# The query work of a fused attention and relu² kernel planned by session, and the copy of its sums set between two subtractions

## The chip, the cores and the metric

The kernel runs on one core of a Trainium2 chip. The metric is the device time of one execution in microseconds (us). Runs of the kernel before the change took 1959.41 to 1961.84 us. TensorE is called PE in the profile (PEld is its weight load), VectorE is DVE, ScalarE is ACT, GpSimd is POOL, and SyncE, whose queue issues all the DMAs here, is SP.

## The reference, cut to what matters

```python
# q, k, v: 4 x 12480 x 128; agents: 4 x 49 x 128; w_in: 128 x 2048; w_out: 2048 x 128
def sm(a, b):                                   # softmax of scaled scores
    s = scale * (a @ b.transpose(0, 2, 1))
    e = np.exp(s - s.max(-1, keepdims=True))
    return e / (e.sum(-1, keepdims=True) + 1e-9)
agent_v = sm(agents, k) @ v                     # 4 x 49 x 128
x = (sm(q, agents) @ agent_v).reshape(49920, 128)
h = np.maximum(x @ w_in, 0)
return (h * h) @ w_out
```

The work has two parts for each of the four batches. A small table comes from agents, keys, values and `w_in`: the product of `agent_v` with `w_in`, 49 rows of 2048. Then each token needs only its 49 softmax weights times that table, relu, square, and the product with `w_out`.

## The kernel before, in words

The 49920 tokens are 52 blocks of 960 (13 to a batch), and a block is two halves of G = 480 tokens. The 2048 hidden units are 16 chunks of 128, and a slot is two of them for one half, so a half has 8 slots and a block 16. Slots are taken in sessions of 3, 3 and 2 (`SIZES`; the first half of all has four sessions of 2, `EARLY`). In what follows the three sessions of a half are called A, B (three slots each) and C (two slots).

A session `s` does this, in the order of the loop at the end of the kernel. `first` issues the matmuls `h<-w,aw_hi` and `h<-x,aw_ex` of its slots into PSUM and ACT's relu `r<-h` behind them. ACT squares `r` in place (`squares`). `halved` splits the squares of the session before into a rounded part `g_hi` (a cast on DVE) and a rest `g_lo` (a subtraction on DVE). `second` issues, for the session two before (`LAG` = 2), six matmuls a slot into the sum `o`: four with `g_hi` and then, when all of these are out, two with `g_lo`. So PE's order is first(s), second(s-2), first(s+1), second(s-1), and so on: first(A), second(B of the half before), first(B), second(C of the half before), first(C), second(A).

The sum `o` has one PSUM bank. When the second(C) that ends a half is out, `copied_out` copies `o` to `ob` on DVE and sends it to memory; the next half's second(A) may write `o` only when that copy is done. Before the change `copied_out` is called in the session after, so that on DVE the copy stands behind the whole subtraction `g_lo` of session A and ahead of the cast of session B.

Two kinds of work lie beside these sessions. Both are generators, advanced a step at a time: `queries(g)` (the softmax weights of block `g`) and `background(b)` (the table of the next batch from its keys and values; the last batch has none to prepare). Both use one PSUM bank `psa`, one user at a time, and a step of the background that a session takes stands between that session's first and second on PE. The steps of `queries(g)`:

- the load of the block's queries (`qt`);
- the scores `psa<-ag,qt` on PE, with the row maxima `m` and the difference `e` on DVE (L317, L319);
- the exponential on ACT (L323);
- the sums, reciprocal and product on DVE (L326 to L329);
- the cast `pp` on ACT (L227) and its rest on DVE (L229);
- for each half j: four matmuls `psa<-identr,pp`, called transposes below, and the cast `w<-psa` on ACT; in the step after, one DMA `w<-w` (L346) and four DMAs `x<-w` (L348).

Relu, square, the cast `w<-psa`, `g_hi`, `g_lo`, the copy `ob` and all of these matmuls are issued through `queued`, which fixes their order on their engine. The other DVE, ACT and DMA instructions are placed among them by the framework's scheduler.

Before the change `between(k)`, `first` and `due()` decide when the queries advance: the scores of block g+1 in session A of the first half of block g, the steps after it one at each slot, the transposes of j = 0 at the end of A and those of j = 1 at the end of B in the second half of block g. The DMAs follow a slot later.

Of the kernel before, what the change touches and what calls it, by code (L numbers as in the profile page):

```python
# [9 lines left out]
F32 = mybir.dt.float32  # L10
# [13 lines left out]
SIZES = (3, 3, 2)  # L24
EARLY = (2, 2, 2, 2)
WIDEST = max(SIZES)
# [3 lines left out]
LAG = 2  # L30
# [7 lines left out]
BEGIN = 4  # L38
FIRST = 7
# [3 lines left out]
def agent_attention_relu2(ctx: ExitStack, tc: tile.TileContext, qT, kT, v, agT, w_in, w_out, outT):  # L43
# [26 lines left out]
    class Ordered:  # L70
        def __init__(self, eng, always=False):
            self.eng, self.always = eng, always
# [179 lines left out]
    def values(b, i, vt):  # L252
        st = state[b]
        _, rows, nt = blocks[i]
        es = st["mx"][:rows, :nt, :]
        e = small.tile([P, NT, NA], F32, name="d", bufs=2)[:rows, :nt, :] if i else es
        less_maximum(b, i, e, spare())
        yield
        act.activation(e, e, AF.Exp, scale=scale)
        yield 3 if i else FIRST  # L260
        pv = bank()
        for t in range(nt):
            tiled(pv[:C, :NA], vt[:rows, t, :], e[:, t, :], start=(t == 0), stop=(t == nt - 1))
        if i == 0:
            st["av"] = small.tile([C, NA], F32, name="av")
            dve.tensor_copy(st["av"], pv[:C, :NA])
        else:
            dve.tensor_add(st["av"], st["av"], pv[:C, :NA])  # L268
            spare().tensor_add(es, es, e)
# [20 lines left out]
                sync.dma_start(ex[t * 32 : t * 32 + NL, n, :].bitcast(F32), lo[SP:, t * P : (t + 1) * P].bitcast(F32))  # L290


    class Turn:
        def __init__(self, wait):
            self.session = session[0] + wait

    def due():
        at = stands.get("ahead")
        return isinstance(at, Turn) and session[0] >= at.session

    session = [0]
    weights = {}
    slot = [0]

    def queries(g):
        b = g // NB
        qt = qp.tile([C, BLK], F32, name="qt", bufs=1)
        sync.dma_start(qt, qT[:, g * BLK : (g + 1) * BLK])
        yield 3
        ps = ps_a.tile([P, 512], F32, name="psa")  # L310
        sv = ps[:TP, : NT * NA].rearrange("p (t a) -> p t a", a=NA)
        for t in range(NT):
            tiled(sv[:, t, :], qt[:, t * TP : (t + 1) * TP], ag[:, b, :])
        if alone[0]:
            yield
        m = qp.tile([TP, NT, 1], F32, name="m", bufs=1)
        dve.reduce_max(m, sv, axis=AX.X)  # L317
        e = qp.tile([TP, NT, NA], F32, name="e", bufs=1)
        dve.tensor_sub(e, sv, m.broadcast_to([TP, NT, NA]))  # L319
        yield  # L320
        if not alone[0]:
            yield
        act.activation(e, e, AF.Exp, scale=scale)  # L323
        yield
        z = qp.tile([TP, NT, 1], F32, name="z", bufs=1)
        dve.reduce_sum(z, e, axis=AX.X)  # L326
        dve.tensor_scalar_add(z, z, 1e-9)  # L327
        dve.reciprocal(z, z)
        spare().tensor_mul(e, e, z.broadcast_to([TP, NT, NA]))  # L329
        yield  # L330
        pp = qp.tile([TP, NT, K2], F32R, name="pp", bufs=1)
        yield from halves(pp, e, NA, spare())
        weights[g] = []
        for j in range(2):
            yield Turn(0 if j or slot[0] < SLOTS else 2)
            pt = ps_a.tile([P, 512], F32, name="psa")
            for t in range(NT // 2):
                queued(
                    nc.tensor.matmul, nc.tensor, pt[:K2, t * TP : (t + 1) * TP], pp[:, j * (NT // 2) + t, :], identr, start=True, stop=True
                )  # L340
            w = qp.tile([P, G], F32R, name=f"w{j}", bufs=2)
            x = qp.tile([P, G], F32R, name=f"x{j}", bufs=2)
            fixed.copy(w[:K2, :], pt[:K2, :G])
            weights[g].append((w, x))
            yield
            sync.dma_start(w[K2:, :].bitcast(F32), w[:SP, :].bitcast(F32))  # L346
            for t in range(NQ):
                sync.dma_start(x[t * 32 : t * 32 + NL, :].bitcast(F32), w[SP:NA, :].bitcast(F32))  # L348
# [9 lines left out]
    def first(k, m):  # L358

        g, i = divmod(k, SLOTS)  # L360
        j, c = divmod(i, NP)
        b = g // NB
        w, x = weights[g][j]
        hs = [ps_h.tile([P, 2, 512], F32, name="h") for _ in range(m)]
        outs = [(2 * c + n, hs[n // 2][:, n % 2, :G]) for n in range(2 * m)]
        for n, out in outs:
            cs = slice(n * P, (n + 1) * P)
            queued(nc.tensor.matmul, nc.tensor, out, state[b]["hi"][:, cs], w, start=True, stop=False)

        with tc.high_priority():  # L370
            for n, out in outs:
                t = n % NQ
                rows = slice(t * 32, t * 32 + NL)
                queued(nc.tensor.matmul, nc.tensor, out, state[b]["lo"][rows, n // NQ, :], x[rows, :], start=False, stop=True)
        r = ffn.tile([P, WIDEST, 2, G], F32, name="r", bufs=RB)
        for x, h in enumerate(hs):
            queued(nc.scalar.activation, nc.scalar, r[:, x, :, :], h[:, :, :G], AF.Relu)
        for name in ("ahead", "todo"):
            if (m == WIDEST or not due()) and type(stands.get(name)) is int and k >= stands[name] and done[name] < goal[name]:
                move(name, k)  # L380
                break
        return r

    def squares(m, r, apart):
# [6 lines left out]
    def halved(k, m, r, apart):  # L391
        hi = ffn.tile([P, WIDEST, 2, G], F32R, name="g_hi", bufs=HB)
        lo = ffn.tile([P, WIDEST, 2, G], F32R, name="g_lo", bufs=LB)
        for x in pieces(m, apart):
            queued(nc.vector.tensor_copy, nc.vector, hi[:, x, :, :], r[:, x, :, :])
        for x in pieces(m, apart):
            queued(nc.vector.tensor_sub, nc.vector, lo[:, x, :, :], r[:, x, :, :], hi[:, x, :, :].bitcast(F32))
        for x in range(m):
            parts[k + x] = hi[:, x, :, :], lo[:, x, :, :]

    whole_sum = []

# [55 lines left out]
            return next(gen, "end")  # L458

    gens, stands = {}, {}  # L460
    done, goal = {"todo": 0, "ahead": 0}, {"ahead": math.inf}

    def move(name, k):
        done[name] += 1
        said = step(gens[name])
        stands[name] = k + said if type(said) is int else said
# [54 lines left out]
    with tc.tile_pool(name="pre", bufs=PRE) as pre, tc.tile_pool(name="dec", bufs=2) as dec:  # L521
# [48 lines left out]
        asks(2 * FF - WIDE)  # L570
        ahead = queries(1)
        next(ahead)
        gens["todo"], gens["ahead"] = background(1), ahead
        next(gens["todo"])
        stands["todo"], done["todo"], stands["ahead"] = None, 1, BEGIN

        mx = pre.tile([P, 512], F32, name="mx0", bufs=1)
        ss = []
# [121 lines left out]
    def between(k):  # L700
        g, c = divmod(k, SLOTS)
        b, i = divmod(g, NB)
        slot[0] = k
        if b > 0 and i == 0 and c == 0 and b + 1 < B:
            gens["todo"] = background(b + 1)
            stands["todo"], done["todo"] = None, 0
        goal["todo"] = (i * SLOTS + c + 1) * STEPS / (SPREAD * NB * SLOTS) if k >= BEGIN else 0
        while done["todo"] < goal["todo"] and stands["todo"] is None:
            move("todo", k)
        if c == SLOTS // 2 and g < B * NB - 2:  # L710
            following[0] = queries(g + 2)
            step(following[0])
        if c == 0 and 0 < g < B * NB - 1:
            gens["ahead"], stands["ahead"] = following[0], k
        if stands["ahead"] is None and k > 0:
            move("ahead", k)

    following = [None]
    sessions, at = [], 0
    while at < total:  # L720
        for m in SIZES if at else EARLY:
            sessions.append((at, m))
            at += m
    made, split = {}, {}
    for s in range(len(sessions) + LAG):
        k, m = sessions[s] if s < len(sessions) else (total, 0)
        session[0] = s
        if s == LAG:
            behind = [chain[eng] for eng in (nc.tensor, nc.sync, nc.scalar, nc.vector, nc.gpsimd)]
        if m:  # L730
            between(k)
            made[s] = first(k, m)
        copied_out()
        if m:
            squares(m, made[s], s < LAG)
            if s < LAG:
                alone[0] = True
                if s:
                    warm(ps_a, 5)
                table(s + 2)  # L740
                alone[0] = False
        if 1 <= s <= len(sessions):
            halved(*sessions[s - 1], made.pop(s - 1), s <= LAG)
        if s >= LAG:
            second(*sessions[s - LAG])
            if due():
                move("ahead", slot[0])
        for x in range(1, m):
            between(k + x)
    copied_out()  # L750


_NAMES = ["qT", "kT", "v", "agT", "w_in", "w_out"]
# [32 lines left out]
```

## Time and profile before

| what | value |
|---|---|
| median of 3 runs | 1960.92 us |
| profiled execution, its own time | 1959.76 us |
| its span (first to last instruction) | 1957.7 us |
| PE busy | 1902.4 us (97% of the span) |
| PEld busy | 1479.6 us (76%) |
| DVE busy | 1641.2 us (84%) |
| ACT busy | 1628.1 us (83%) |
| mean granted TensorE clock | 0.996 of full speed |

The span is what the trace covers; the profiled execution took 2.1 us more than it. Busy time is the time in which at least one instruction of the engine is running, so 1957.7 less 1902.4 is the time in which PE ran no matmul. Lines of helpers (L64) hold most instructions, so that groups are told apart by their tiles.

### The profile page before, as it was taken

The numbers are of one execution on the slowest core, as the hardware profiler recorded it, in microseconds if no ns is written. First come the engines' busy times: TensorE is split into PE (matmuls) and PEld (weight loads), VectorE is DVE, ScalarE is ACT, GpSimd is POOL, SyncE is SP. The second block draws the span as 40 slices with busy tenths as digits, with TensorE's granted clock in tenths as the row PEclk, the third lists the DMA queues.
The fourth block names the chain that finished last, engine by engine and source line by source line (L and its number), as shares of the span: only waits on it lengthen the run. The fifth ranks groups of instructions, "written<-read, shape, count | busy, mean of one in ns | idle before, by whom it ended". The sixth has DMA issues, their size and how long they took to land.

```text
span 1957.7 us, 39753 instructions
## 1 busy us (share of the span) xinstructions
PE 1902.4 (97%) x17181; PEld 1479.6 (76%) x17181; DVE 1641.2 (84%) x1371; ACT 1628.1 (83%) x1516; POOL 20.7 (1%) x24
## 2 busy tenths in 40 slices
PE   7899999999999999999999999999999999999999
PEld 4677777777777777777777777777777777777777
DVE  7778888888888888888888888888888888888887
ACT  5778788888888888888888888888888888889886
POOL 2100000000000000000000000000000000000000
PEclk9999999999999999999999999999999999999999
DMA  9222122122122222122112221222111111111100
GB/s 373 78 87 90 55 62 78 62 65 68 37 64 91 72 64 73 56 74 67 56 47 74 78 76 41 67 72 75 47 39 51 36 51 34 45 43 40 47 22 27
DMA packets 54819, 131.47 MB, mean 67 GB/s; under 512 B 6508, under 2 KB 34828, under 8 KB 54644
## 3 DMA queue, kind: packets, MB, share of 16 engines
q1 hardware_dynamic: 54644, 128.93, 20.3%
q8 instruction: 135, 2.21, 0.5%
q14 instruction: 40, 0.33, 0.1%
HBM read 80.97 MB, written 25.56 MB: 54 GB/s over the span
## 4 chain that ended last, share of the span: by engine, by line
PE 65%; ACT 16%; DVE 11%; issue 7%; DMA 1%; SPq 0%; ACTq 0%; DVEq 0%
PE o L64 40%; PE h L64 19%; ACT r L64 15%; PE psa L64 5%; DVE g_hi L64 4%; DVE g_lo L64 4%; DVE ob L64 1%; DMA ahead<-in_kT 0%; DVE t L64 0%; DVE mx L64 0%; ACT w L64 0%; DMA x<-w 0%; DVE d L235 0%; DVE rest L64 0%; DVE z L327 0%
## 5 line engine op out<-in xcount | busy, mean ns | idle before, releaser
L64 ACT ACTIVATE r<-h 128x960 f32<-128x960 f32 x832 | 755.3, 974 | 277.9 <-PE h L64 277.9
L64 DVE TENSOR_TENSOR g_lo<-r,g_hi 128x2880 fp32r<-128x2880 f32 (+2 forms) x315 | 880.6, 2796 | 16.6 <-DVE g_hi L64 0.9
L64 ACT ACTIVATE r<-r 128x2880 f32<-128x2880 f32 (+2 forms) x315 | 734.1, 2331 | 8.3
L64 PE MATMUL o<-g_hi,wo_lo 128*128 128x480 f32 x1664 | 669.2, 402 | 17.4 <-DVE ob L64 16.7
L64 DVE CAST g_hi<-r 128x2880 fp32r<-128x2880 f32 (+2 forms) x315 | 465.2, 1477 | 262.5 <-ACT r L64 258.8
L64 PE MATMUL o<-g_hi,wo_hi 128*128 128x480 f32 x1664 | 632.6, 380 | 0.0
L64 PE MATMUL h<-w,aw_hi 128*128 128x480 f32 x1664 | 419.5, 383 | 0.4 <-DVE aw_hi L64 0.4
L64 PE MATMUL o<-g_lo,wo_hi 128*128 128x480 f32 x1664 | 413.0, 380 | 0.0
L64 PEld LDWEIGHTS o<-g_hi,wo_lo 128*128 128x128 f32 x1664 | 313.6, 188 | 118.1 <-DVE ob L64 32.9
L64 PEld LDWEIGHTS o<-g_lo,wo_hi 128*128 128x128 f32 x1664 | 313.9, 189 | 48.9
L64 PEld LDWEIGHTS o<-g_hi,wo_hi 128*128 128x128 f32 x1664 | 314.1, 189 | 42.3 <-issue 2.9
L64 PEld LDWEIGHTS h<-w,aw_hi 128*128 128x128 f32 x1664 | 304.7, 188 | 45.6 <-DVE aw_hi L64 1.7
L64 PE MATMUL h<-x,aw_ex 19*128 19x480 f32 x1664 | 198.8, 455 | 2.3 <-DMA x<-w 2.3
L64 PEld LDWEIGHTS h<-x,aw_ex 19*128 19x128 f32 x1664 | 82.1, 182 | 108.1 <-issue 104.4
L64 DVE COPY ob<-o 128x480 f32<-128x480 f32 x104 | 67.5, 649 | 2.1 <-PE o L64 2.1
L64 PEld LDWEIGHTS psa<-identr,pp 120*98 120x98 f32 x416 | 51.0, 165 | 18.7 <-DVE av L268 3.8
L64 ACT CAST w<-psa 98x480 fp32r<-98x480 f32 x104 | 56.8, 546 | 1.8 <-PE psa L64 1.0
L64 PE MATMUL psa<-identr,pp 120*98 120x120 f32 x416 | 51.1, 245 | 5.8 <-DVE aw_lo L283 2.3
L64 PEld LDWEIGHTS psa<-ag,qt 128*32 128x32 f32 (+1 forms) x3328 | 40.6, 110 | 20.0 <-issue 16.0
L64 PE MATMUL psa<-ag,qt 128*32 128x49 f32 (+1 forms) x3328 | 47.8, 211 | 2.5 <-DVE aw_hi L64 2.5
L64 PEld LDWEIGHTS psa<-ag,kt 128*32 128x32 f32 x2340 | 28.2, 110 | 16.6 <-ACT w L64 6.5
L64 PEld LDWEIGHTS psa<-d,vt 128*32 128x32 f32 (+1 forms) x2160 | 26.4, 109 | 19.0 <-ACT w L64 8.9
(138 smaller groups left out, 628.4 us busy)
## 6 DMA issues: line engine op xcount, KB each, us to landing
qt<-in_qT SPq DMA_DIRECT2D x52, 480.0 KB
out_T<-ob SPq DMA_DIRECT2D x104, 240.0 KB
kt<-in_kT SPq DMA_DIRECT2D x36, 512.0 KB
vt<-in_v SPq DMA_DIRECT2D x36, 512.0 KB
x<-w SPq DMA_DIRECT2D x416, 35.6 KB
ahead<-in_kT SPq DMA_DIRECT2D x12, 512.0 KB
ahead<-in_v SPq DMA_DIRECT2D x12, 512.0 KB
w<-w SPq DMA_DIRECT2D x104, 56.2 KB
```

What stands on the lines that cost most here:

```text
L64: ins = issue(*args, **kw)
```

## The change

Three things. First, the mechanism that moved the queries along slot by slot (`Turn`, `due`, `slot`, `following`, the name "ahead") is replaced by a table `plan`, written before the loop, that names for each step of `queries(g)` a session and a place in it: "start" (ahead of everything), "block" (behind relu, where otherwise the background takes its step), "mid" (behind the second slot's turn of the background) or "end" (behind `second`). From block 3 on the query load is at the start of block g-2, the scores in session A of its second half, the exponential in its last session, the sums, the product and the cast in A of block g-1, the rest in B; the transposes of j = 0 come at the end of C of the first half of block g-1 and those of j = 1 at the end of C of its second half, each with its DMAs at the start of the session after. Blocks 1 and 2 have lists of their own.

Second, `copied_out` moves from the session after to the very session that ends the half, behind its `second`. Where a session ends a half, the subtraction `g_lo` (of session A) is split: all slots but the last ahead of the copy, the last one behind it.

Third, the first step of `values` waits 2 slots where it waited 3, and a step without work is gone from `queries`.

```diff
-        yield 3 if i else FIRST
+        yield 2 if i else FIRST
...
-        if not alone[0]:
-            yield
...
-            yield Turn(0 if j or slot[0] < SLOTS else 2)
+            yield
...
-        for name in ("ahead", "todo"):
-            if (m == WIDEST or not due()) and type(stands.get(name)) is int and k >= stands[name] and done[name] < goal[name]:
-                move(name, k)
-                break
+        if not planned("block") and type(stands["todo"]) is int and k >= stands["todo"] and done["todo"] < goal["todo"]:
+            move("todo", k)
...
-        for x in pieces(m, apart):
-            queued(nc.vector.tensor_sub, nc.vector, lo[:, x, :, :], r[:, x, :, :], hi[:, x, :, :].bitcast(F32))
         for x in range(m):
             parts[k + x] = hi[:, x, :, :], lo[:, x, :, :]
+        return r, hi, lo
+
+    def rests(r, hi, lo, some):
+        for x in some:
+            queued(nc.vector.tensor_sub, nc.vector, lo[:, x, :, :], r[:, x, :, :], hi[:, x, :, :].bitcast(F32))
...
+    S = len(SIZES)
+    for g in range(1, B * NB):
+        this, before = starts[g], starts[g - 1]
+        gen = queries(g) if g > 1 else ahead
+        if g == 1:
+            plans(
+                gen, (LAG, "block"), (LAG + 1, "start"), (LAG + 1, "mid"), (LAG + 2, "start"), (LAG + 2, "mid"),
+                (this - 2, "end"), (this - 1, "start"), (this - 1, "end"), (this, "start"),
+            )
+            continue
+        if g == 2:
+            plans(gen, (LAG + 1, "start"), (before - 1, "block"), (before, "start"), (before, "mid"))
+            plans(gen, (before + 1, "start"), (before + 1, "mid"))
+        else:
+            first_of = starts[g - 2]
+            plans(gen, (first_of, "start"), (first_of + S, "block"), (before - 1, "start"), (before, "start"))
+            plans(gen, (before, "mid"), (before + 1, "start"))
+        plans(gen, (before + S - 1, "end"), (before + S, "start"), (this - 1, "end"), (this, "start"))
+
+    def planned(phase):
+        todo = plan.pop((now[0], phase), ())
+        for gen in todo:
+            step(gen)
+        return bool(todo)
...
         if m:
+            planned("start")
             between(k)
             made[s] = first(k, m)
-        copied_out()
-        if m:
             squares(m, made[s], s < LAG)
...
         if 1 <= s <= len(sessions):
-            halved(*sessions[s - 1], made.pop(s - 1), s <= LAG)
+            n = sessions[s - 1][1]
+            split = halved(*sessions[s - 1], made.pop(s - 1), s <= LAG)
+            ends = s >= LAG and sum(sessions[s - LAG]) % NP == 0
+            if s <= LAG:
+                some = pieces(n, True)
+            else:
+                some = [slice(0, n - 1), slice(n - 1, n)] if ends else [slice(0, n)]
+            rests(*split, some[:1] if ends else some)
         if s >= LAG:
             second(*sessions[s - LAG])
-            if due():
-                move("ahead", slot[0])
-        for x in range(1, m):
+            copied_out()
+            if ends and s <= len(sessions):
+                rests(*split, some[1:])
+            planned("end")
+        if m:
+            between(k + 1)
+            planned("mid")
+        for x in range(2, m):
             between(k + x)
-    copied_out()
```

## Rows read from the trace of the kernel before

**Rows 1.** Busy time by stretch: stretch and its length, then each engine, clock, DMA.

```profile
1000.00:1480.00 480.00, 469.50 (x4602) 367.88 (x4601) 406.19 (x339) 402.97 (x371) 0.00 (x0) 1.00 0.20 62
1480.00:1940.00 460.00, 457.29 (x3031) 357.45 (x3030) 393.20 (x280) 403.32 (x348) 0.00 (x0) 1.00 0.12 39
```

**Rows 2.** Waits of the whole span: waiter, released by, us, times, longest.

```profile
DVE g_hi L64 <- ACT r L64: 258.8, 175, 2.9
...
PE o L64 <- DVE ob L64: 16.7, 33, 1.4
...
PE psa L64 <- ACT w L64: 11.8, 12, 1.2
...
PE psa L64 <- DVE aw_lo L283: 2.3, 3, 0.8
PE h L64 <- DMA x<-w: 2.3, 3, 1.0
...
PE psa L64 <- DVE mb L222: 2.1, 3, 0.7
...
PE psa L64 <- DVE av L268: 1.4, 6, 0.3
```

**Rows 3.** PE's timeline at a half's end, last batch: start, us, instruction, [idle].

```profile
1890.14 1.04 PE L64 MATMUL o<-g_lo,wo_hi 128*128 128x480 f32 x4
1891.02 1.02 PE L64 MATMUL h<-w,aw_hi 128*128 128x480 f32 x4
1891.97 0.49 PE L64 MATMUL h<-x,aw_ex 19*128 19x480 f32 x4
1892.62 0.49 PE L64 MATMUL o<-g_hi,wo_lo 128*128 128x480 f32 x1 [0.17 <-DVE ob L64]
1895.34 1.47 PE L64 MATMUL o<-g_lo,wo_hi 128*128 128x480 f32 x6
```

**Rows 4.** DVE's timeline over the same half's end.

```profile
1886.73 1.66 DVE L64 CAST g_hi<-r 128x2880 fp32r<-128x2880 f32 x1 [1.26 <-ACT r L64]
...
1888.78 3.15 DVE L64 TENSOR_TENSOR g_lo<-r,g_hi 128x2880 fp32r<-128x2880 f32 x1
...
1891.92 0.65 DVE L64 COPY ob<-o 128x480 f32<-128x480 f32 x1
...
1893.55 1.66 DVE L64 CAST g_hi<-r 128x2880 fp32r<-128x2880 f32 x1 [0.28 <-ACT r L64]
```

**Rows 5.** PE's timeline in the last block, which has no transposes.

```profile
1926.44 0.48 PE L64 MATMUL o<-g_hi,wo_lo 128*128 128x480 f32 x1 [0.64 <-DVE ob L64]
```

**Rows 6.** Groups by shape: busy, mean ns of one, idle before.

```profile
L64 DVE TENSOR_TENSOR g_lo<-r,g_hi 128x2880 fp32r<-128x2880 f32 x206 | 649.7, 3154 | 6.7 <-DVE g_hi L64 0.5
...
L64 DVE TENSOR_TENSOR g_lo<-r,g_hi 128x1920 fp32r<-128x1920 f32 x105 | 226.5, 2157 | 9.9 <-DVE g_hi L64 0.5
```

**Rows 7.** PE's timeline behind the transposes at an end of session B.

```profile
1165.61 0.48 PE L64 MATMUL psa<-identr,pp 120*98 120x120 f32 x4
...
1168.03 0.90 PE L64 MATMUL psa<-ag,kt 128*32 128x49 f32 x64 [0.60 <-ACT w L64]
```

**Rows 8.** ACT's timeline over the same transposes.

```profile
1167.41 0.57 ACT L64 CAST w<-psa 98x480 fp32r<-98x480 f32 x1
```

**Rows 9.** ACT's timeline from the square of a C to the next relu.

```profile
1878.38 1.81 ACT L64 ACTIVATE r<-r 128x1920 f32<-128x1920 f32 x1
1881.35 2.71 ACT L64 ACTIVATE r<-h 128x960 f32<-128x960 f32 x3 [1.16 <-PE h L64]
```

**Rows 10.** DVE's timeline ahead of a copy while values of the background run.

```profile
1259.54 0.20 DVE L268 TENSOR_TENSOR av<-av,psa 128x49 f32<-128x49 f32 x1
...
1260.85 0.65 DVE L64 COPY ob<-o 128x480 f32<-128x480 f32 x1
```

**Rows 11.** PE's timeline at the start of block 1.

```profile
102.36 0.77 PE L64 MATMUL h<-x,aw_ex 19*128 19x480 f32 x3 [0.71 <-DMA x<-w]
```

**Rows 12.** ACT's timeline: the cast whose rows block 1 waits for.

```profile
92.28 0.54 ACT L64 CAST w<-psa 98x480 fp32r<-98x480 f32 x1
```

**Rows 13.** Busy time around that wait.

```profile
98.00:106.00 8.00, 5.73 (x77) 3.58 (x76) 3.66 (x4) 3.78 (x4) 0.00 (x0) 0.67 0.17 38
```

More of the change, by code (lines that the diff above doesn't have):

```diff
@@ L290, in tables @@
                 sync.dma_start(ex[t * 32 : t * 32 + NL, n, :].bitcast(F32), lo[SP:, t * P : (t + 1) * P].bitcast(F32))
[L293 to L301, printed above, removed]
     weights = {}
-    slot = [0]
+    now = [0]
     def queries(g):
@@ L460, in agent_attention_relu2 @@
     gens, stands = {}, {}
-    done, goal = {"todo": 0, "ahead": 0}, {"ahead": math.inf}
+    done, goal = {"todo": 0}, {}
     def move(name, k):
@@ L572, in agent_attention_relu2 @@
         next(ahead)
-        gens["todo"], gens["ahead"] = background(1), ahead
+        gens["todo"] = background(1)
         next(gens["todo"])
-        stands["todo"], done["todo"], stands["ahead"] = None, 1, BEGIN
+        stands["todo"], done["todo"] = None, 1
         mx = pre.tile([P, 512], F32, name="mx0", bufs=1)
@@ L702, in between @@
         b, i = divmod(g, NB)
-        slot[0] = k
         if b > 0 and i == 0 and c == 0 and b + 1 < B:
@@ L709, in between @@
             move("todo", k)
[L710 to L719, printed above, removed]
+    sessions, starts, at = [], [], 0
     while at < total:
+        if at % SLOTS == 0:
+            starts.append(len(sessions))
         for m in SIZES if at else EARLY:
@@ L723, in agent_attention_relu2, with plans @@
             at += m
-    made, split = {}, {}
+    plan = {}
+    def plans(gen, *whens):
+        for at, phase in whens:
+            plan.setdefault((at, phase), []).append(gen)
+    S = len(SIZES)
[21 more added lines that the diff above has]
+        return bool(todo)
+    made = {}
     for s in range(len(sessions) + LAG):
         k, m = sessions[s] if s < len(sessions) else (total, 0)
-        session[0] = s
+        now[0] = s
         if s == LAG:
```

## The prediction

> **What bounds the kernel now.** I read the busy times by stretch first. With the background running, PE is busy 469.50 of 480 us, and in the last batch, which has no background, 457.29 of 460; the clock is granted in full in both, and DVE and ACT are busy for 85 to 88% [rows 1]. So the kernel ends when PE has worked through its fixed order, and a change that takes no matmul away can win only the time in which PE stands idle. Over the span that is 1957.7 - 1902.4 = 55.3 us, part of it in the start-up before the sessions.
>
> The list of waits says what that idle time waits for, and the reader should look only at the lines whose waiter is PE [rows 2]. Behind the start-up there are three sorts. PE waits for the copy `ob` 33 times, 16.7 us: the next half may not write the bank `o` before. It waits for the cast `w` 12 times, 11.8 us: the next user of `psa` stands behind the transposes. And 12 times, 2.3 + 2.1 + 1.4 = 5.8 us, it waits for DVE to release `psa` (`aw_lo`, `mb`, `av`), mostly at the transposes. Together these are 34.3 us. A fourth line is the wait of block 1 for its DMAs `x<-w`, 2.3 us. The 258.8 us that DVE waits for ACT show the other side: DVE has slack, some 2.5 us to each of the 104 halves, in which it waits for squares.
>
> **The copy.** The timeline at a quiet half's end shows how the copy comes late. PE's last matmul of second(C) ends at 1890.14 + 1.04 = 1891.18, and the first matmul of the next half starts at 1892.62, after 0.17 idle; its turn came when `h<-x` ended, at 1891.97 + 0.49 = 1892.46, or some hundredths before, as neighbours overlap [rows 3]. On DVE the subtraction of session A runs from 1888.78 to 1891.93 and the copy from 1891.92 to 1892.57 [rows 4]. So the sum was ready 0.74 us before DVE took it up. With the split, two slots of the subtraction take 2.16 us [rows 6], to 1890.94; the copy can then start when PE is done, at about 1891.2, and is over at 1891.9. That is 0.5 us ahead of PE's turn in place of 0.1 behind.
>
> A slot more costs 3.154 - 2.157 = 1.00 us, so an instruction's fixed part is 3.154 - 3 x 1.00 = 0.16 us and the last slot alone takes 1.16 us (an estimate from two sizes) [rows 6]. The split adds 104 x 0.16 = 17 us to DVE. I cost it at nothing on the end: what hides it is DVE's wait for ACT. After copy and last slot DVE is free at about 1893.1, and the cast of session B waited for its square until 1893.55 anyway [rows 4], so 0.45 us of cover is left. Gone, the cast would be later by the excess, and its reader on PE comes a whole session later. The other reader is nearer: PE wants the last slot of `g_lo` 16 matmuls into second(A), at (1895.34 - 1892.62)/12 = 0.23 us each some 3.6 us after 1892.4, so at 1896.0 [rows 3], about 3 us after DVE has it.
>
> With the background DVE is later. The rows at 1259.54 show an `av` step behind the subtraction and the copy only at 1260.85 [rows 10]; between them stand the background's difference and the queries' reciprocal and product. The plan takes the queries' steps out of that place: the sums and product go to the start of A, where DVE has only a two-slot session to split. So the copy gains up to 1.0 us from the split and loses up to about 0.8 us of such work ahead of it. The longest wait is 1.4 us [rows 2]. I take 15 of the 16.7 us as won; the ends are 8 (if the background's DVE steps fill the new gap each time) and 16.7. In the last block, where no transposes stand at an end of B, the wait for the copy is 0.64 us [rows 5]. The plan makes every half like that one, so without the move of the copy the first part of the change would have lengthened these waits.
>
> **The transposes.** At an end of B they cost 0.32 us of PE and keep doing so elsewhere. What follows them is what counts: the transposes start at 1165.61, ACT takes up the cast `w` at 1167.41 and ends it at 1167.98, and the scores at 1168.03 wait 0.60 us for it [rows 7, 8]. ACT is behind there because B is its full session, relu and square of three slots, against PE's second of two. After C it is the other way: the square ends at 1880.19 and the next relu waits for PE until 1881.35, 1.16 us of idle ACT [rows 9], in which a cast of 0.57 us fits. The next user of `psa` stands behind a first(A) of three slots: first(C) takes 1.44 us for two [rows 3], so about 2.1 us. The cast is done 1.5 us before its reader. I take all 11.8 us.
>
> The releases of `psa` by DVE (5.8 us, at most 0.8 each [rows 2]) go too: a step of the background in the same session uses the bank just ahead of second, and at an end of C that is second(A) with 18 matmuls, six more than second(C), so 1.3 us later. Ends: nothing won, if a release slips behind a subtraction of 3.15 us, and 5.8.
>
> **The other moves.** The exponential, the sums and the casts are the same instructions in other sessions; they lie beside PE. The DMAs are as many; SP is passed by nothing new except that the copy's own store is issued about a microsecond sooner. Their lead matters: the one late landing that the trace shows is block 1's, whose cast ended at 92.82 and whose last row was there at 102.36, 9.5 us later [rows 11, 12]. Both DMAs of later blocks now have half a block, about 1957.7/104 = 18.8 us. Block 1's own list keeps its places, so its wait stays, with the slow clock around it (0.67 granted [rows 13]); block 2's scores move from behind that wait to before it, worth 0 to 2 us, and I take 0. The shorter first step of `values` and the empty step cost nothing: no instruction goes.
>
> **The sum.** 15.0 + 11.8 + 5.8 = 32.6 us. Against it I set 4 us of new waits, 0.1 us for each of the 39 blocks that carry background: the cover at the copy is only half a microsecond. That leaves 28.6, and 1959.76 - 28.6 = 1931.2. The profiled execution lies 1.2 us below the median of 1960.92, inside the spread of the three, so I say 1931. At best everything goes, 34.3 us, and with it the part of each of 57 waits that overlapping matmuls hide (`h<-x` at 1891.97 starts 0.07 us before its predecessor ends at 1892.04 [rows 3]; 57 x 0.07 = 4.0) and 1 to 2 us of start-up: 1920.
>
> **The rivals.**
>
> *Half of it.* One of the two parts works and the other's waits only change place. If the copy stays late (the scheduler fills the gap ahead of it with the background's steps), 11.8 + 5.8 less 4 remain, to which 1 to 4 us of the copy's may come: 1942 to 1946. If the bank `psa` is as contended at the ends of C, 15 less up to 4 remain: 1945 to 1949. For it: one bank serves both generators still. Against it: the 1.16 us on ACT, and the 0.74 us by which the sum lay ready.
>
> *No change.* PE's idle time comes back as waits for squares, because ACT or DVE is the true bound: about 1960. Against it: both are idle 12 to 15% and wait for PE or each other [rows 1, 2], and no line of PE waiting for a cast `g_hi` in a full session is among the long ones.
>
> *Slower: the copy blocks its queue.* The copy now waits on DVE for PE, and what stands behind it waits along: the last slot of the subtraction, the cast of B, and whichever unchained DVE steps were placed there. If one of these reads `psa` for a background step taken in B, the bank is free only after copy, last slot and cast, 0.65 + 1.16 + about 0.5 + 1.66 + 0.2 = 4.2 us after second(C), where the step in C wants it after 1.44 us [rows 3, 4, 10]: 2.8 us of PE each. By the code a batch's background has 33 users of `psa`, 20 of them with a reader on DVE, and a third of sessions are Bs, so about 20 such cases in three batches: 56 us, less 28.6, gives 1987. It decides from 28.6/20 = 1.4 us a case on. Against it: in the rows the reader stands ahead of the copy [rows 10], and its data are there before the two-slot subtraction ends.
> The Trainium skill ("TensorE: Matmul & The Clock Gate", "Architectural detail") says that VectorE and ScalarE work their queues strictly in order, where TensorE may pull weight loads forward; by that rule nothing overtakes a waiting copy, so that its price would be this rival's 1987 wherever a reader stands behind it. The trace agrees as far as it goes, since each DVE row starts where the one before ends.
>
> **How the numbers follow.** The forecast, 1921 to 1938, has 0.67: its three waits are read off directly, and each has its cover in a row. Half of it, 1939 to 1950, has 0.18; no change 0.06; slower 0.09. The range 1921 to 1950 takes in the first two and leaves out 0.15. About 0.2%, some 4 us, is what a measurement of this kernel can tell from no change: faster 0.85, same 0.06, slower 0.09.
>
> **What would show it.** Right: the lines of PE waiting for `ob`, `w`, `mb`, `av`, `aw_lo` shrink to a few microseconds together, PE's busy time stays near 1902 and the span falls by what they lose; the copy stands between two subtractions and starts as second(C) ends, with DVE waiting for PE there; the cast `w` stands in ACT's gap behind the square of C; the wait for `x<-w` at block 1 remains. Wrong: PE waiting at the transposes for a DVE reader, at `o` for the copy or for the last `g_lo`, or at `h` for the relu of C; a lower granted clock; `x<-w` late in later blocks.

## The result and the profile after

The changed kernel takes 1932.78 us (median of 4 runs, 1931.26 to 1933.27), against 1960.18 us before: a ratio of 0.9858, 95% interval 0.9841 to 0.9875. The forecast was 1931. The profiled execution took 1933.27 us, its span is 1931.4, that is 26.3 less than the 1957.7 of before.

The busy times of the changed kernel, first the page's line for the whole span, then three stretches with the background running, of which the last is that of [rows 1]:

```profile
PE 1899.9 (98%) x17181; PEld 1481.4 (77%) x17181; DVE 1652.5 (86%) x1474; ACT 1633.3 (85%) x1516; POOL 20.7 (1%) x24
```
```profile
140.00:530.00 390.00, 386.33 (x3761) 303.02 (x3761) 336.07 (x305) 331.67 (x302) 0.00 (x0) 1.00 0.22 67
530.00:1000.00 470.00, 466.40 (x4590) 366.52 (x4585) 405.85 (x364) 402.97 (x368) 0.00 (x0) 1.00 0.21 67
1000.00:1480.00 480.00, 476.34 (x4639) 374.13 (x4639) 416.37 (x374) 411.04 (x376) 0.00 (x0) 1.00 0.20 64
```

PE's idle time is 1931.4 - 1899.9 = 31.5 us, where it was 55.3: 23.8 of the 26.3 us. The other 2.5 are in busy time that got shorter. The mean granted clock is 0.996 in both kernels, so the clock is not what shortened it; the cause was not traced. With the background running, PE is now busy for 99%: 476.34 of 480 us in the last stretch, against 469.50 before. The list of waits says which idle time went. The lines of the changed kernel that answer to [rows 2]:

```profile
DVE g_hi L64 <- ACT r L64: 218.0, 148, 3.1
...
PE psa L64 <- DVE aw_lo L283: 9.7, 6, 1.7
...
DVE ob L64 <- PE o L64: 6.3, 16, 1.3
...
PE psa L64 <- ACT w L64: 1.5, 1, 1.5
...
PE o L64 <- DVE ob L64: 1.2, 3, 0.4
...
PE h L64 <- DMA x<-w: 0.3, 1, 0.3
```

The waits for `ob` fell from 16.7 to 1.2 us, those for the cast `w` from 11.8 to 1.5 (the one left stands in the start-up), those of block 1 for its DMAs from 2.3 to 0.3. The lines for `mb` and `av` are gone. But `aw_lo` grew from 2.3 to 9.7 us, six waits of 1.5 to 1.7. DVE now waits for PE at the copy, 6.3 us in 16 places.

A quiet half's end in the changed kernel, PE and then DVE, to be laid beside [rows 3, 4]:

```profile
1882.12 1.04 PE L64 MATMUL o<-g_lo,wo_hi 128*128 128x480 f32 x4
1882.99 1.02 PE L64 MATMUL h<-w,aw_hi 128*128 128x480 f32 x4
1883.95 0.49 PE L64 MATMUL h<-x,aw_ex 19*128 19x480 f32 x4
1884.36 0.48 PE L64 MATMUL o<-g_hi,wo_lo 128*128 128x480 f32 x1
```
```profile
1881.27 2.16 DVE L64 TENSOR_TENSOR g_lo<-r,g_hi 128x1920 fp32r<-128x1920 f32 x1
1883.34 0.65 DVE L64 COPY ob<-o 128x480 f32<-128x480 f32 x1
1883.91 1.15 DVE L64 TENSOR_TENSOR g_lo<-r,g_hi 128x960 fp32r<-128x960 f32 x1
1885.53 1.66 DVE L64 CAST g_hi<-r 128x2880 fp32r<-128x2880 f32 x1 [0.47 <-ACT r L64]
```

The copy stands between the two subtractions, is over at 1883.99, and PE's first matmul of the next half starts at 1884.36 with no wait; before, in the same kind of place, it waited 0.17 us, and in the last block 0.64 [rows 3, 5]. The last slot takes 1.15 us, and the cast of B still waits for its square.

With the background running, the queries' steps still stand ahead of the copy. DVE over one such half's end, and PE's first matmul of the next half:

```profile
1253.60 2.15 DVE L64 TENSOR_TENSOR g_lo<-r,g_hi 128x1920 fp32r<-128x1920 f32 x1
...
1256.56 0.57 DVE L318 TENSOR_TENSOR e<-e,z 120x392 f32<-120x392 f32 x1
1257.05 0.65 DVE L64 COPY ob<-o 128x480 f32<-128x480 f32 x1
```
```profile
1258.10 0.48 PE L64 MATMUL o<-g_hi,wo_lo 128*128 128x480 f32 x1
```

`e<-e,z` is the queries' product. In the trace it stands between the subtraction and the copy at 49 of the 104 ends of a half, where it was 27 before: the plan issues it in session A, and on DVE it comes only behind the subtraction of that session's slots. The copy is in time all the same, 0.40 us ahead of PE here, since the subtraction ahead of it is a slot shorter.

### The profile page after: what moved, and what is told of

It is laid out like the page before. It is cut to its first block, busy times and chain, and to the rows that moved or that the text cites. A ratio compares the mean times of both kernels' runs of the same rounds, so it can differ in the third digit from the quotient of the medians.

```text
span 1931.4 us, 39943 instructions
## 1 busy us (share of the span) xinstructions
PE 1899.9 (98%) x17181; PEld 1481.4 (77%) x17181; DVE 1652.5 (86%) x1474; ACT 1633.3 (85%) x1516; POOL 20.7 (1%) x24
## 4 chain that ended last, share of the span: by engine, by line
PE 92%; DVE 3%; ACT 3%; issue 1%; DMA 1%; SPq 0%; POOL 0%; DVEq 0%; POOLq 0%; ACTq 0%
PE o L64 57%; PE h L64 27%; PE psa L64 8%; ACT r L64 2%; DMA ahead<-in_kT 0%; DVE g_lo L64 0%; DVE t L64 0%; DVE g_hi L64 0%; DVE mx L64 0%; DMA x<-w 0%; DVE rest L64 0%; DVE aw_lo L283 0%; SPq L64 0%; DVE ob L64 0%; ACT s L64 0%
## 5 line engine op out<-in xcount | busy, mean ns | idle before, releaser
L64 DVE TENSOR_TENSOR g_lo<-r,g_hi 128x1920 fp32r<-128x1920 f32 (+2 forms) x418 | 896.1, 2144 | 12.2
L64 PE MATMUL psa<-identr,pp 120*98 120x120 f32 x416 | 50.7, 244 | 10.3 <-DVE aw_lo L283 9.7
```

The lines of the kernel that those rows point to most:

```text
L64: ins = issue(*args, **kw)
```

## The experiments

Kernels of one group shared the runs of the kernel before, whose medians were 1960.02 to 1960.60 us.

**The plan alone.** The copy goes back to the session after, and the subtraction is whole again.

```diff
         if m:
             planned("start")
             between(k)
             made[s] = first(k, m)
+        copied_out()
+        if m:
             squares(m, made[s], s < LAG)
...
-                some = [slice(0, n - 1), slice(n - 1, n)] if ends else [slice(0, n)]
-            rests(*split, some[:1] if ends else some)
+                some = [slice(0, n)]
+            rests(*split, some)
         if s >= LAG:
             second(*sessions[s - LAG])
-            copied_out()
-            if ends and s <= len(sessions):
-                rests(*split, some[1:])
             planned("end")
```

> The plan alone: queries by session, the copy and the whole subtraction as before the change. Theory 1 (the two parts need each other: with no transposes at an end of B, PE comes earlier to the bank o, and the copy behind three slots of subtraction is late): PE waits for ob in most halves whose sessions A and B carry no other PE work, 30 to 60 times at 0.3 to 0.7 us, 20 to 35 us in all, in place of 1.2; time 1950 to 1965 us, little better than before. Theory 2 (the plan does the work, the copy's place matters little): 1931 to 1940 us, PE's waits for ob under 8 us.

1967.95 us, ratio 1.0042 (1.0026 to 1.0059): slower than before, and 3 us above theory 1's range. PE's waits for the copy are 25.4 us, as theory 1 has them, and the six for `aw_lo` are there too; together these are more than the plan wins. The waits of this kernel:

```profile
PE o L64 <- DVE ob L64: 25.4, 48, 1.0
PE psa L64 <- DVE aw_lo L283: 9.7, 6, 1.7
```

**The copy alone.** The kernel before with the split subtraction and the copy of the changed kernel.

```diff
-            halved(*sessions[s - 1], made.pop(s - 1), s <= LAG)
+            split = halved(*sessions[s - 1], made.pop(s - 1), s <= LAG)
+            rests(*split, some[:1] if ends else some)
         if s >= LAG:
             second(*sessions[s - LAG])
+            copied_out()
+            if ends and s <= len(sessions):
+                rests(*split, some[1:])
             if due():
                 move("ahead", slot[0])
```

> The copy alone: split subtraction and copy in the session that ends the half, queries as before the change. Theory 1 (waits add up; each part wins the waits it is meant for): PE's waits for ob fall from 16.7 to under 3 us, those for the cast w (11.8 us) and for releases of psa by DVE (5.8 us) stay; time 1943 to 1948 us. Theory 2 (the plan does the work): 1955 to 1961 us.

1939.44 us, ratio 0.9896 (0.9881 to 0.9911), better than theory 1 by 4 us. In this kernel the cast `w` costs what it did, the copy 4.7 us (under 3 were expected), and the releases of `psa` 0.8 us instead of 5.8:

```profile
PE psa L64 <- ACT w L64: 11.8, 12, 1.2
PE o L64 <- DVE ob L64: 4.7, 9, 0.8
...
PE psa L64 <- DVE aw_lo L283: 0.8, 3, 0.3
```

So the copy's part wins most of the releases as well, although the transposes stand where they stood.

**No split.** The changed kernel with the whole subtraction ahead of the copy.

```diff
-                some = [slice(0, n - 1), slice(n - 1, n)] if ends else [slice(0, n)]
+                some = [slice(0, n)]
```

> The changed kernel with the whole subtraction ahead of the copy; the copy is still issued in the session that ends the half. Theory 1 (it is the split that frees the copy): like the plan alone, PE waits 20 to 35 us for ob, 1950 to 1965 us. Theory 2 (it is the issue in the half's own session, ahead of the unchained DVE steps that stood before the copy): ob waits under 8 us, 1932 to 1940 us.

1965.92 us, ratio 1.0036 (1.0024 to 1.0049), with 25.6 us of waits for `ob`: the same as the plan alone, and just above theory 1's range. Issuing the copy in the half's own session wins nothing by itself; what frees it is that subtraction work goes behind it.

**The copy first.** The changed kernel with all three slots of the subtraction behind the copy.

```diff
-                some = [slice(0, n - 1), slice(n - 1, n)] if ends else [slice(0, n)]
-            rests(*split, some[:1] if ends else some)
+                some = [slice(0, n)]
+            rests(*split, some[:0] if ends else some)
...
-                rests(*split, some[1:])
+                rests(*split, some)
```

> The changed kernel with the whole subtraction of A behind the copy, so that DVE waits for PE about 2 us in each half and then has 3.15 us of subtraction to do in one piece. Theory 1 (a waiting copy holds DVE's queue, and half a microsecond of cover is all there is): the cast of B comes about 1.6 us later, DVE's slack of 2.1 us a half is used up where the background runs, and PE waits for g_lo or for a release of psa; 1940 to 1975 us. Theory 2 (DVE's order around the copy is free as long as the copy is early): 1930 to 1935 us.

1921.17 us, ratio 0.9803 (0.9788 to 0.9817): the fastest kernel of the study, 12 us ahead of the changed one, and better than either theory. Theory 1 is wrong: DVE waits for PE 152.1 us, where it had waited for ACT, and PE waits 0.9 us for `g_lo`. The waits of this kernel:

```profile
DVE ob L64 <- PE o L64: 152.1, 98, 2.7
DVE g_hi L64 <- ACT r L64: 51.9, 85, 1.9
...
PE o L64 <- DVE g_lo L64: 0.9, 4, 0.3
```

There is no line for `aw_lo` left. Why is seen in DVE's order. First the changed kernel, then this one, each from the cast of a B on DVE, with ACT's `aw_hi` beside it, to PE's transposes behind the C:

```profile
513.86 1.66 DVE L64 CAST g_hi<-r 128x2880 fp32r<-128x2880 f32 x1 [0.62 <-ACT r L64]
515.56 3.16 DVE L64 TENSOR_TENSOR g_lo<-r,g_hi 128x2880 fp32r<-128x2880 f32 x1
518.64 0.73 DVE L283 SCALAR_TENSOR_TENSOR aw_lo<-psa,rl,aw_hi 49x512 fp32r<-49x512 f32 x1
```
```profile
515.44 0.69 ACT L64 ACTIVATE aw_hi<-psa,rl 98x512 fp32r<-98x512 f32 x1
```
```profile
519.42 0.56 PE L64 MATMUL psa<-identr,pp 120*98 120x120 f32 x4 [1.69 <-DVE aw_lo L283]
519.82 2.00 PE L64 MATMUL h<-w,aw_hi 128*128 128x480 f32 x6
```
```profile
513.16 1.66 DVE L64 CAST g_hi<-r 128x2880 fp32r<-128x2880 f32 x1
514.73 0.74 DVE L283 SCALAR_TENSOR_TENSOR aw_lo<-psa,rl,aw_hi 49x512 fp32r<-49x512 f32 x1
515.39 3.14 DVE L64 TENSOR_TENSOR g_lo<-r,g_hi 128x2880 fp32r<-128x2880 f32 x1
```
```profile
513.43 0.69 ACT L64 ACTIVATE aw_hi<-psa,rl 98x512 fp32r<-98x512 f32 x1
```
```profile
515.57 0.50 PE L64 MATMUL psa<-identr,pp 120*98 120x120 f32 x4
```

In the changed kernel the table's rest, the last reader of `psa`, stands behind 3.16 us of subtraction, and the transposes wait 1.69 us for it. With the copy first, the scheduler put the rest between cast and subtraction. The rest reads `aw_hi`. In the changed kernel that is over at 516.13, after the subtraction has begun; with the copy first it is over at 514.12, before the cast ends at 514.82. Against PE the cast comes later there: 2.4 us ahead of the transposes, where it is 3.9 us ahead in the other kernel, not counting the wait.

The profiled executions of the two kernels differ by 12.9 us of span. PE's idle time gives 9.1 of them (31.5 against 22.4), about what the six waits cost, and busy time 3.8. The clock has part in the busy time: the changed kernel ran two stretches at the lower clock, 94 to 98 us (0.58 granted) and 521 to 524 (0.50, shown in the last section), and with the copy first the same places are granted in full.

**The table's rest early.** Is it that order, and not the copy's place, that is worth the 12 us? In this run the copy and the split are as in the changed kernel, and the rest is put into DVE's fixed order between cast and subtraction.

```diff
     def rests(r, hi, lo, some):
+        while late:
+            queued(nc.vector.scalar_tensor_tensor, nc.vector, **late.pop(0))
         for x in some:
...
-            dve.scalar_tensor_tensor(
+            late.append(dict(
                 out=lo, in0=pw[:NA, :], scalar=rl[:NA, :], in1=hi[:NA, cs].bitcast(F32),
                 op0=ALU.mult, op1=ALU.subtract,
-            )
+            ))
```

> The changed kernel with the table's rest aw_lo (the DVE reader that holds psa in the six longest waits left) queued on DVE between the cast of a session and its subtraction, in place of where the scheduler put it, behind a subtraction of 3.15 us. Theory 1 (PE's waits add to the time one for one): the six waits of 9.7 us go, PE idles some 21 us in all, 1922 to 1926 us. Theory 2 (the wait is only passed on, to the subtraction behind it and PE's g_lo): 1930 to 1934 us.

1926.70 us, ratio 0.9827 (0.9812 to 0.9843): half of the 12 us. The six waits are gone, but in sessions B the rest now stands ahead of the copy, and PE's waits for `ob` rise from 1.2 to 6.1 us:

```profile
PE o L64 <- DVE ob L64: 6.1, 6, 1.6
```

In three of these places the rest waits for `aw_hi` (1.58 to 1.63 us in the trace) and holds the subtraction and the copy behind it. So neither theory holds whole: 9.7 us went and 4.9 came back. With the copy first the rest comes early and nothing holds the copy; that these two together make the 12 us fits the waits of both kernels, and no run takes them further apart.

**The old places of the transposes.** The changed kernel, copy and split kept, with the transposes at the ends of A and B of the second half.

```diff
-        plans(gen, (before + S - 1, "end"), (before + S, "start"), (this - 1, "end"), (this, "start"))
+        plans(gen, (before + S, "end"), (before + S + 1, "start"), (before + S + 1, "end"), (before + S + 2, "start"))
```

> The changed kernel, copy and split kept, but the transposes at the ends of A and B of the second half, where they stood before the change, each with its DMAs a session later. Theory 1 (the place of the transposes decides, by ACT's gap behind C): PE waits for the cast w 10 to 12 us again, and 3 to 6 us for DVE to release psa; the 9.7 us of waits for aw_lo at the ends of C shrink to about 2; time 1936 to 1943 us. Theory 2 (the place does not matter once the copy is early): 1923 to 1933 us.

1939.02 us, ratio 0.9884 (0.9866 to 0.9901), in theory 1's range. The waits for the cast `w` are back, more of them than before the change, and those for `aw_lo` shrink:

```profile
PE psa L64 <- ACT w L64: 16.0, 18, 1.5
...
PE o L64 <- DVE ob L64: 2.5, 6, 0.4
...
PE psa L64 <- DVE aw_lo L283: 0.8, 3, 0.3
```

The new ends are worth 1939.0 - 1932.8 = 6.2 us here: some 14 us of the cast, less 9 of `aw_lo`. Three of the waits for the cast are followed by a lower clock in the profiled execution (last section), which adds to their price.

**The plan with the old ends and the old copy.** The edit just shown, on the plan alone.

> The plan with the transposes at the ends of A and B of the second half, and the copy and the whole subtraction as before the change. Theory 1 (the new ends are what makes the late copy hurt, since PE loses the transposes that it had to do while the copy came): PE waits for ob fall from 25 us to 8 to 18, for w 11 to 17 us are back; 1955 to 1963 us, like before the change. Theory 2 (something else in the plan, the steps of the queries in other sessions, makes the copy late): ob waits stay over 20 us, 1968 to 1980 us.

1962.80 us, ratio 1.0014 (1.0005 to 1.0023), 0.1% above before and in theory 1's range. But the waits for `ob` are above its 8 to 18, over 20 as theory 2 has them:

```profile
PE o L64 <- DVE ob L64: 21.2, 42, 1.4
...
PE psa L64 <- DVE aw_lo L283: 3.3, 3, 1.1
```

So 4.2 us of the 25.4 are due to the new ends, and the other half of the step, from 16.7 to 21.2, lies in the plan's other moves; which of them, was not taken apart.

**The copy first, without the plan.** The kernel before with the copy ahead of the whole subtraction.

> The copy ahead of the whole subtraction of A, with the queries planned as before the change. Theory 1 (the copy wins its own 16.7 us, and the plan is worth the 11.8 us that PE waits for the cast w and little else): PE waits for ob under 1 us, for w 10 to 13 us; 1934 to 1941 us, that is 13 to 20 us behind the same copy under the new plan. Theory 2 (with a copy this early the plan is worth nothing): 1919 to 1926 us.

1952.06 us, ratio 0.9956 (0.9940 to 0.9973): 31 us behind the same copy under the new plan, more than theory 1 has, and 13 behind the split copy with the old plan. Neither theory's range holds it. The cast `w` costs 11.8 us as expected, but here the subtraction is late, and DVE waits for ACT:

```profile
DVE pp L229 <- ACT pp L227: 60.3, 47, 3.0
...
PE psa L64 <- ACT w L64: 11.8, 12, 1.2
...
PE o L64 <- DVE g_lo L64: 4.7, 24, 0.3
```

With the old plan the queries' rest `pp` (L229), which reads ACT's cast `pp`, often stands directly ahead of the copy, at 36 of the 104 ends of a half (at one with the new plan). In the last batch DVE waits there for ACT, as from 1571.59 to 1573.03; the copy follows at 1573.51, 0.64 us after second(C) ended, and the subtraction behind it is late. So a step that waits ahead of the copy takes back what its early place gives. That `pp` accounts for the whole difference is not shown. Of the 31.6 us between the two spans, 20.4 are idle time of PE and 11.2 busy time; where the busy time comes from was not traced.

The median times of the two parts together, in us:

| copy | queries as before | queries by the plan |
|---|---|---|
| behind the subtraction | 1960.0 | 1968.0 |
| between two subtractions | 1939.4 | 1932.8 |
| ahead of the subtraction | 1952.1 | 1921.2 |

**The first step of values.** It waits 3 slots again, as before the change.

```diff
-        yield 2 if i else FIRST
+        yield 3 if i else FIRST
```

> The changed kernel with the first step of values waiting 3 slots, as before the change. Theory 1 (the shorter wait costs and wins nothing, since no instruction goes): 1931 to 1935 us. Theory 2 (it sets which session of a half the background's values fall in, and 3 slots put their readers where they delay the copy or the transposes): 1937 to 1945 us.

1932.16 us, ratio 0.9851 (0.9834 to 0.9869), in theory 1's range, with the same waits: this edit costs and wins nothing that can be measured.

**Block 2's scores behind the wait of block 1.** A single run, for the start-up.

```diff
-            plans(gen, (LAG + 1, "start"), (before - 1, "block"), (before, "start"), (before, "mid"))
-            plans(gen, (before + 1, "start"), (before + 1, "mid"))
+            plans(gen, (LAG + 1, "start"), (before, "block"), (before + 1, "start"), (before + 1, "mid"))
+            plans(gen, (before + 2, "start"), (before + 2, "mid"))
```

> The changed kernel with the scores of block 2 behind the wait of block 1 for its DMAs, in A of block 1, as before the change, and their later steps a session later. One look, to be read at the start of block 1. Theory 1 (scores ahead of the wait fill it, and keep the clock up): the waits for x<-w grow from 0.3 to over 2 us again, the clock between 98 and 106 us is granted in part, and the second session of block 1 starts 1 to 2.5 us later than in the changed kernel (107.99 us). Theory 2 (the earlier landing comes from the store issued sooner): x<-w waits stay under 1 us and that session starts within 0.5 us of 107.99.

The one time is 1935.15 us. The waits for `x<-w` are 2.2 us again, and the clock falls around them, as theory 1 has it. Its second session of block 1 starts at 111.56, 3.6 us after that of the changed kernel; 0.7 of that it had lost before the place in question (the `h<-x` of session 5 starts at 87.04 against 86.33), and the 2.9 that are left are above theory 1's 2.5. The busy time around the wait, first in this kernel:

```profile
98.00:106.00 8.00, 5.83 (x85) 4.14 (x84) 4.02 (x5) 3.12 (x4) 0.00 (x0) 0.80 0.31 93
```

Then in the changed kernel, over the stretch before and the same stretch:

```profile
94.00:98.00 4.00, 4.00 (x12) 3.36 (x13) 3.96 (x3) 2.51 (x2) 0.00 (x0) 0.58 0.26 47
98.00:106.00 8.00, 7.17 (x97) 5.36 (x96) 5.44 (x8) 4.56 (x8) 0.00 (x0) 1.00 0.28 86
```

The kernel before had 0.67 from 98 to 106 [rows 13]. In the changed kernel the lower clock has not gone; it comes earlier, behind a wait of 1.51 us for the cast `w`, and lasts for less time.

## Why the prediction was right, by its steps

**The copy: right in size and in the main mechanism.** 15 us were taken as won; the profile after shows 16.7 - 1.2 = 15.5. Putting the subtraction back ahead of the copy brings 25.6 us of waits. That the first part without the second would have lengthened these waits was said, and the plan alone is 8 us slower than the kernel before; but the reason given, that no transposes stand at an end of B, accounts for 4.2 of the 8.7 us that these waits grew by. One premise did not come: the plan was to take the queries' steps out of the place ahead of the copy, and the rows at 1256.56 and 1257.05 show the product still there. The split alone made the copy early enough. DVE waits for PE at 16 copies only; in the quiet half shown it takes the copy up 0.18 us after second(C) ends, 0.37 us of lead are left where 0.5 were forecast, and the cast of B has 0.47 us of cover where 0.45 were. The cover turned out not to matter: with the copy first DVE waits some 1.5 us a half (152.1/104), its cast of B has no slack left in the quiet halves, and what follows for PE is 0.9 us of waits for `g_lo`. What PE reads of that cast is a session away, as the prediction itself had it.

**The cast `w`: right.** 11.8 us were taken; 10.3 went, and one wait of 1.5 us appeared in the start-up, where block 2's scores now stand close behind the transposes. Moving these scores away does not win it: in that run the scores of the keys stand there and wait 1.52 us. With the old ends the cast costs 16.0 us. ACT's timeline in the changed kernel shows the cast in the gap behind the square of a C, with 1.19 us still idle before the next relu:

```profile
1887.25 1.82 ACT L64 ACTIVATE r<-r 128x1920 f32<-128x1920 f32 x1
1888.96 0.54 ACT L64 CAST w<-psa 98x480 fp32r<-98x480 f32 x1
1890.69 2.70 ACT L64 ACTIVATE r<-h 128x960 f32<-128x960 f32 x3 [1.19 <-PE h L64]
```

**The releases of `psa`: the term that failed.** 5.8 us were taken as won by the new ends, on the ground that second(A) gives DVE 1.3 us more. In the changed kernel they cost 9.7 us, 3.9 more than before, so they came out below even the lower end, nothing won. That end named the reason, "a release slips behind a subtraction of 3.15 us", and that is what the rows at 515.56 and 518.64 show; I gave it too little weight, since in [rows 10] the reader stood well placed. PE waiting at the transposes for a DVE reader was also listed as a sign of being wrong. The other runs show the rest. With the old ends the releases fall to 0.8 us as soon as the copy is early, with the old plan and with the new (with the copy late and the new plan they are 3.3 for `aw_lo` and 1.9 for `m`); with the new ends `aw_lo` costs 9.7 us whether the copy is late or split. So it was the copy's part that won what the new ends were credited with, and the new ends lost it again to `aw_lo`.

**The new waits: right as a sum, wrong as a place.** 4 us were set for some tenths at each block with background. What came is 9.7 - 2.3 = 7.4 us at `aw_lo`, two waits in each of three batches. These are the waits of the term above, so they count once.

**The start-up: 0 taken of 0 to 2.** From the `h<-x` of session 5 to the second session of block 1 it takes 107.99 - 86.33 = 21.7 us, against 109.89 - 86.19 = 23.7 before: 2.0 won, at the upper end. The run with block 2's scores late ties it to their place, by one execution. The prediction had also said that the wait for `x<-w` stays; it fell to 0.3 us.

So the sum is right to 2 us because errors cancel, and that closeness is luck: 32.6 less 4 was written, and the trace has 15.5 + 10.3 - 3.9 for the three sorts of waits, which is 21.9, then 2.0 at the wait of block 1 and some 2.5 of busy time that no term foresaw. One reading was a little off: with the background ACT is busy for 402.97 of 480 us, 84% and not 85. **The rivals:** no change is out by 27 us. Half of it is not what happened, although each part by itself is far from its share: the plan alone +8, the copy alone -21, together -27. The slower rival, a waiting copy that holds its queue, has its mechanism in the rows (DVE does wait there, in order), but the forced version of it, with the copy first, is the fastest kernel. With the old plan it costs 13 us against the split, but there DVE waits for ACT ahead of the copy as well. No case of a `psa` reader stuck behind the copy showed in the list of waits of the changed kernel; the reader that was stuck stood behind a subtraction.

## What to carry to other kernels

When one engine is busy for 97% of the span, add up what its idle pieces wait for; that sum, and not the busy shares of the others, says about what a reordering can win (34.3 us here, where the fastest kernel won 38.9). A result that frees a bank should be taken up soon after it is complete, and work that is due later goes behind it. On an engine with slack even an idle wait for it can be cheap, but what stands around the copy decides: the copy first was the fastest with the new plan, and slower than the split with the old. And two reorderings should be tried together and apart, since the second can be a loss without the first; readers of a shared bank that a scheduler places freely deserve a fixed place, between short instructions, and then a look at what they now delay.

## What the runs showed of the hardware that was not expected

A single wait can cost more than itself. Behind one of the six waits for `aw_lo`, of 1.69 us, PE fell from 2.4 to 1.2 GHz: the granted clock is 0.50 from 521 to 524 us. The six matmuls `h<-w` behind the transposes take 2.00 us, where those at 506.57 take 1.46; with `h<-x` (1.17 against 0.70) and the scores (1.44 against 0.90) that is 1.6 us, about the wait again. The busy time of that stretch in the changed kernel:

```profile
521.00:524.00 3.00, 3.00 (x66) 1.80 (x68) 1.70 (x1) 1.41 (x2) 0.00 (x0) 0.50 0.11 29
```

Ahead of it PE had run the matmuls of `g_lo` to their end and then waited. The other five waits, of 1.52 to 1.72 us, have no stretch of lower clock near them in this profile. The same six waits stand in four other kernels. There the clock fell behind the same second wait in two (the plan alone, and the values that wait 3 slots) and nowhere in the other two.

Shorter waits are followed by it too. With the transposes at the ends of A and B, three of the 18 waits for the cast `w`, of 1.13, 1.16 and 1.20 us, have such a stretch behind them, the first of them this one, behind the wait that ends at 245.16:

```profile
246.00:249.00 3.00, 3.00 (x9) 2.51 (x8) 3.00 (x4) 2.97 (x3) 0.00 (x0) 0.50 0.14 42
```

So the length of a wait alone does not say whether the clock falls behind it; what else decides was not tested.
